# The second expert layer's weights and tokens from expert 2 on: three products of fp32r halves, split on the chip, in place of one fp32 product

## The chip, the cores and the metric

The kernel runs on one core of a Trainium2 chip, as a single launch. The metric is the device time of that launch in microseconds (us). Before the change, three timed runs gave 1102.97, 1103.93 and 1105.5 us; their median is 1103.93 us.

A core has five engines that work side by side, each through its own list of instructions in order: PE (matrix products; its weight loads are shown apart as PEld), DVE (elementwise and reductions, the vector engine), ACT (elementwise, the scalar engine), POOL and SP (here mostly issuers of DMAs). They wait for one another through semaphores. PE writes its products to PSUM, eight banks of 128 partitions by 512 fp32 columns; all else stands in SBUF.

## What is computed

Three stages follow one another. Only the last is touched.

```
x = attention(q, k, v)                 # 4 x 12 heads x 448 x 64 -> x[1792, 768]
x = moe(x)                             # each token to the expert of its largest logit
# the third stage, moe2:
logits = x @ w_gate                    # [1792, 8]
# all 14336 pairs (token, expert) by falling logit; a pair is taken if the token
# is free and the expert has fewer than 224 tokens
for e in range(8):
    mask = assigned == e               # exactly 224 tokens
    h = np.maximum(x[mask] @ w1[e], 0.0)   # 224x768 @ 768x1024
    out[mask] = h @ w2[e]                  # 224x1024 @ 1024x768
```

All tensors are fp32, the weights of an expert are 3 MB + 3 MB.

## The kernel before

Attention takes the first third of the span, the first expert layer (`moe1`) the second, the assignment and the second expert layer (`moe2`, L1961) the last. Already in `moe1` every fp32 operand is split into two numbers of the type fp32r: a high half (`w1h`, `xh`: the operand rounded to fp32r, an ACT copy, L846) and a low half (`w1l`, `xl`: operand minus high half, a DVE subtraction, L847). A product is then the sum of three, high x high, high x low and low x high (L880 to L882, L908 to L911).

`moe2` used plain fp32 products, an instruction each, which stands in the trace as two PE records. It works through the eight experts in the order in which the assignment fills them. Per expert n:

- First layer: for each of 8 blocks f of 128 hidden units, 6 products (`acc`, L2076; k = 0..5, 128 weights columns by the 224 tokens `xtt`) add up in one of two PSUM banks, f % 2 (`product`), so that block f+2 needs the bank that block f has left. `relu` (L2080) is one ACT instruction, PSUM to `ht`.
- Second layer: for each half h of the tokens (112), 8 x 2 products of 384 columns (`gemm2`, L2090) add up in two banks. `store` (L2095, L2096) copies them out by ACT and scatters the rows by a POOL DMA; half 0 is stored at step t = 25 of the expert, half 1 at step t = 3 of the next.
- The next expert's rows are gathered by POOL (L2056), and transposed by PE in four `turn`s during the second layer (L2064; ACT copies them to `xtt`, L2068).
- Weights: `pump` (L2027) issues one DMA for each piece, 6 of 512 KB (first layer) and 8 of 384 KB (second), straight into one of two sets of fp32 buffers, `w1s` and `w2s`; the next expert's pieces go into the other set.

The order of the instructions is made while the program is built. A small model of the engines' clocks (`Pace`, with `work(engine, cost, not before)`) decides only between which products the steps of the assignment (`asn`, DVE and PE work on 128 partitions, to which all of L1615 to L1955 belong) are put. All of `experts` is written out twice, for two variants of the assignment, of which one runs.

Of the kernel before, what the change touches and what calls it, by code (L numbers as in the profile page):

```python
# [1411 lines left out]
CAP = N // E  # L1412
# [545 lines left out]
        return t  # L1958


def moe2(tc, consts, wt, x0, asn, w1, w2, y, out):  # L1961

# [7 lines left out]
    with ExitStack() as ctx:  # L1970
        ctx.enter_context(tc.manual_schedule())
        p2 = ctx.enter_context(tc.tile_pool(name="m2p", bufs=1, reuse_waits="tile"))
        ps = ctx.enter_context(tc.tile_pool(name="m2ps", bufs=1, space=PSUM))
        w1s, w2s = wt
# [5 lines left out]
        xt = p2.tile([128, KD, CAP], F32, name="xtt")  # L1980
        ht = p2.tile([128, KF, CAP], F32, name="ht")
# [40 lines left out]

        nload, firsts, seconds = 0, 0, 0

        there, done = {}, {}  # L2027
# [6 lines left out]
        def pump(most=None):  # L2034
            nonlocal nload
            while most is None or nload < most:
                n, first, k = piece(nload)
                if n >= len(regs) or n > (firsts if first else seconds) + 1:
# [7 lines left out]
                w, wd = (w1, FF) if first else (w2, DM)  # L2046
                clock["d"] = max(clock["d"], clock["p"] + DELAY, choice[n]) + wd * 1.43e-3
                there[n, first, k] = clock["d"]
                nc.sync.dma_start(out=r, in_=w[bass.ds(regs[n], 1), 128 * k : 128 * (k + 1), :].rearrange("a p f -> p (a f)"))
                nload += 1  # L2050

        def gather(n, h):
            clock["d"] = max(clock["d"], work("g", 1.03) + GATHER) + 0.97
# [4 lines left out]
        def turn(g, px=px0):  # L2058
# [8 lines left out]
            there["x", h, i] = work("s", 0.45, t)  # L2067
            nc.scalar.activation(xt[dst], px, AF.Copy)  # L2068

        def acc(n, pg, f, k, shared=False):  # L2070
            fs = slice(128 * f, 128 * f + 128)
            check = dict(skip_group_check=shared)

            t = max(there[n, True, k], there["x", 0, k // 3], there["x", 1, k // 3])
            done[f] = work("p", 0.378, t)
            nc.tensor.matmul(pg, lhsT=w1s[n % 2][:, k, fs], rhs=xt[:, k, :], start=k == 0 and not (shared and f % 2), stop=k == KD - 1, **check)  # L2076

        def relu(pg, f):
            there["h", f] = work("s", 0.38, done[f])
            nc.scalar.activation(ht[:, f, :], pg, AF.Relu)  # L2080

        def gemm2(n, h, t):
            ts = slice(h * CP, (h + 1) * CP)

            todo = [(0, 0), (0, 1)] if t == 0 else [(1, 0), (1, 1)] if t == 1 else [(0, t), (1, t)]
            for i, k in todo:
                po = result(n, h, i)
                work("p", 0.646, max(there[n, False, k], there["h", k]))
                cs = slice(384 * i, 384 * i + 384)
                nc.tensor.matmul(po, lhsT=ht[:, k, ts], rhs=w2s[n % 2][:, k, cs], start=k == 0, stop=k == KF - 1)  # L2090

        def store(n, h):
            work("s", 0.98)
# [12 lines left out]
        nc.gpsimd.memset(w1s[0][0:1, FIRST, 0:1], 0.0)  # L2106
        few = nc.values_load(asn.regs[0:1, E : E + 1], engines=tuple(ALL), min_val=0, max_val=1)
        start = nload, known, list(regs), dict(asn.__dict__)

        def experts(compact):  # L2110
            nonlocal nload, known, firsts, seconds
            nload, known = start[:2]
            firsts, seconds = 0, 0
            regs[:] = start[2]
            choice[:] = [0.0]
            fetched.clear()
            asn.__dict__.update(start[3])
            there.update(((0, True, k), 0.0) for k in range(FIRST))
            pace.start(phases(compact), g=2.0, d=3.5)
            ready.update({0: 4.5, 1: 5.5})  # L2120
            pump()
            turns = [turn(g, (po3 + pg2)[g]) for g in range(4)]
# [6 lines left out]
            for n in range(E):  # L2129
                turns, gathered, turned = [], 0, 0  # L2130

                def ahead(t):

                    nonlocal gathered, turned
                    if n + 1 == E:
                        return
                    if known > n + 1 and gathered < 2:
                        gather(n + 1, gathered)
                        gathered += 1
                    elif t >= 17:  # L2140
                        if turned < 4 and gathered > turned // 2 and ready[turned // 2] <= clock["p"]:
                            if len(turns) == turned:
                                turns.append(turn(turned))
                                next(turns[turned])
                                return
                            for _ in turns[turned]:
                                pass
                            turned += 1

                for t in range(32):  # L2150
                    if n and t % 2 == 0 and 2 <= t <= 16:
                        relu(product(t // 2 - 1), t // 2 - 1)
                    if n and t == 3:
                        store(n - 1, 1)
                    if t == 25:
                        store(n, 0)
                    ahead(t)
                    pump()
                    if t < 16:
                        if n:  # L2160
                            f, a = divmod(t, 2)
                            for k in range(3 * a, 3 * a + 3):
                                acc(n, product(f), f, k)
                        elif t < 6:
# [11 lines left out]
                        if t == 15:  # L2176
                            firsts = n + 1
                    else:
                        gemm2(n, (t - 16) // 8, t % 8)
                seconds = n + 1  # L2180
                if n + 1 == E:
                    break
                while known <= n + 1:
                    clock["p"] = max(clock["p"], pace.step[2])
                    pace.emit()
                pump()
                while turned < 4:
                    if gathered > turned // 2:
                        clock["p"] = max(clock["p"], ready[turned // 2])
                    ahead(17)  # L2190
            store(E - 1, 1)

        with tc.If(few > 0):
            experts(True)
# [6 lines left out]
SLACK = 0.3  # L2201
AHEAD = 0.5
DELAY = 3.2
GATHER = 1.7
FIRST = 1
NHR = 5
# [12 lines left out]
def fused_kernel(tc, q, k, v, g_q, g_k, modality_id, w_gate, bias, w1, w2, w_gate2, w12, w22, out):  # L2219
    nc = tc.nc  # L2220
    with ExitStack() as ctx:
# [31 lines left out]
        wp3 = ctx.enter_context(tc.tile_pool(name="wp3", bufs=1, reuse_waits="tile"))  # L2253
        w1s = [wp3.tile([128, DM // 128, FF], F32, name=f"w1s{i}") for i in range(2)]
        w2s = [wp3.tile([128, FF // 128, DM], F32, name=f"w2s{i}") for i in range(2)]
        moe2(tc, consts, (w1s, w2s), x0, asn, w12, w22, y, out)
# [23 lines left out]
```

## Time and profile before

| what | us |
|---|---|
| median of three runs | 1103.93 |
| profiled execution, its own time | 1102.77 |
| its span (first to last instruction on the core) | 1101.0 |
| PE busy in the span | 1043.8 (95%) |
| DVE busy | 468.5 (43%) |
| ACT busy | 420.9 (38%) |
| mean granted TensorE clock, share of 2.4 GHz | 0.966 |

The profile is one execution, so durations taken from it add up to its span; its own time is 1.77 us above the span, and 1.16 us below the median. Busy shares are means over the three stages, and each stage is to be read by itself; the rows further below are from the stretches that matter here.

### The profile page before, as it was taken

The numbers are of one execution on the slowest core, as the hardware profiler recorded it, in microseconds if no ns is written. First come the engines' busy times: TensorE is split into PE (matmuls) and PEld (weight loads), VectorE is DVE, ScalarE is ACT, GpSimd is POOL, SyncE is SP. The second block draws the span as 40 slices with busy tenths as digits, with TensorE's granted clock in tenths as the row PEclk, the third lists the DMA queues.
The fourth block names the chain that finished last, engine by engine and source line by source line (L and its number), as shares of the span: only waits on it lengthen the run. The fifth ranks groups of instructions, "written<-read, shape, count | busy, mean of one in ns | idle before, by whom it ended". The sixth has DMA issues, their size and how long they took to land. (4 is left out here: it accounts for less than half of the span.)

```text
span 1101.0 us, 18184 instructions
## 1 busy us (share of the span) xinstructions
PE 1043.8 (95%) x6032; PEld 769.6 (70%) x6032; DVE 468.5 (43%) x1460; ACT 420.9 (38%) x995; POOL 233.5 (21%) x228
## 2 busy tenths in 40 slices
PE   7999999999999699999999997859999999999995
PEld 6555556556555688888888986657575886787782
DVE  5777877877875831111311112767777000000000
ACT  3677777677675322122532212721121111111110
POOL 4443333334333500100241101010101011001000
PEclk8899999999999899999999998959999999999998
DMA  6566566565365144627701101055752565376100
GB/s 157 128 145 145 129 149 150 126 156 144 81 175 179 30 147 157 221 97 260 259 22 46 45 30 51 11 181 209 261 196 61 221 229 212 130 251 216 38 13 27
DMA packets 80893, 150.99 MB, mean 137 GB/s; under 512 B 14254, under 2 KB 53422, under 8 KB 80752
## 3 DMA queue, kind: packets, MB, share of 16 engines
q1 hardware_dynamic: 75552, 126.06, 37.5%
q0 software_dynamic: 5200, 23.33, 6.7%
q8 instruction: 54, 0.88, 0.4%
q14 instruction: 87, 0.71, 0.2%
HBM read 110.69 MB, written 17.44 MB: 116 GB/s over the span
## 5 line engine op out<-in xcount | busy, mean ns | idle before, releaser
L2090 PE MATMUL bank<-w2s,ht 128*112 128x384 f32 x512 | 176.5, 490 | 0.0
L2076 PE MATMUL bank<-xtt,w1s 128*128 128x224 f32 x768 | 156.5, 358 | 0.0
L2076 PEld LDWEIGHTS bank<-xtt,w1s 128*128 128x128 f32 x768 | 143.4, 191 | 5.2 <-issue 1.2
L205 DVE TENSOR_REDUCE nm<-sp 112x1 f32<-112x448 f32 x192 | 117.9, 619 | 58.1 <-PE sp L204 29.6
L211 ACT ACTIVATE e<-sp,nm 112x448 f32<-112x448 f32 x192 | 121.8, 634 | 53.2 <-DVE nm L205 34.1
L2090 PEld LDWEIGHTS bank<-w2s,ht 128*112 128x112 f32 x512 | 86.2, 177 | 59.4 <-issue 1.1
L219 PE MATMUL tp<-ident,e 112*112 112x112 f32 x768 | 111.7, 269 | 0.6 <-DVE et L222 0.6
L219 PEld LDWEIGHTS tp<-ident,e 112*112 112x112 f32 x768 | 81.7, 135 | 26.2 <-issue 19.5
L232 PE MATMUL op<-et,qkv 112*64 112x448 f32 x384 | 99.4, 564 | 0.0
L225 ACT ACTIVATE et<-tp 112x448 f32<-112x448 f32 x144 | 78.4, 546 | 37.8 <-PE tp L219 36.3
L2080 ACT ACTIVATE ht<-bank 128x224 f32<-128x224 f32 x64 | 22.4, 357 | 173.0 <-PE bank L2076 166.7
L200 PE MATMUL sp<-bt,at 128*112 128x448 f32 x188 | 85.3, 454 | 1.6 <-DMA bt<-cut 1.6
L908 PE MATMUL po<-w2h,hh 128*128 128x384 f32 x240 | 85.7, 357 | 0.1
L880 PE MATMUL pg<-w1h,xh 128*128 128x512 f32 x180 | 75.9, 422 | 7.1 <-PEq L1192 5.8
L909 PE MATMUL po<-w2l,hh 128*128 128x384 f32 x240 | 81.7, 341 | 0.6 <-DVEq L837 0.5
L911 PE MATMUL po<-w2h,hl 128*128 128x384 f32 x240 | 80.5, 340 | 0.0
L2096 POOL DMA_INDIRECT out_dram<-x,ids x16 | 16.9, 1054 | 294.1 <-ACT x L2095 273.3
L882 PE MATMUL pg<-w1h,xl 128*128 128x512 f32 x180 | 72.2, 401 | 0.0
L881 PE MATMUL pg<-w1l,xh 128*128 128x512 f32 x180 | 72.0, 400 | 0.0
L137 POOL TENSOR_TENSOR xn<-qkv,rr 112x512 f32<-112x512 f32 x47 | 48.0, 1053 | 112.3 <-DVE rr L128 112.3
L200 PEld LDWEIGHTS sp<-bt,at 128*112 128x112 f32 x188 | 33.8, 180 | 48.5 <-issue 31.7
L896 DVE TENSOR_TENSOR hl<-ph,hh 128x512 fp32r<-128x512 f32 x30 | 20.7, 690 | 80.6 <-ACT hh L893 48.8
(417 smaller groups left out, 1550.3 us busy)
## 6 DMA issues: line engine op xcount, KB each, us to landing
w1s<-in_moe_w_dram SPq DMA_DIRECT2D x48, 512.0 KB
w2s<-in_moe_w_dram SPq DMA_DIRECT2D x64, 384.0 KB
qkv<-in_moe_w_dram SPq DMA_DIRECT2D x40, 384.0 KB
raw<-in_moe_w_dram SPq DMA_DIRECT2D x24, 512.0 KB
bt<-cut SPq DMA_DIRECT2D x96, 112.0 KB
at<-cut SPq DMA_DIRECT2D x96, 112.0 KB
qkv<-in_v_dram SPq DMA_DIRECT2D x12, 448.0 KB
xs<-xp SPq DMA_DIRECT2D x24, 224.0 KB
```

The costliest lines, as they stand in the source:

```text
L200: nc.tensor.matmul(sp, lhsT=at[:, h, cs], rhs=bt[:, h, :], start=h == 0, stop=h == 1)
L205: nc.vector.tensor_reduce(out=st["nm"][:, n : n + 1], in_=sp, axis=AX.X, op=OP.max, negate=True)
L211: nc.scalar.activation(e, st.pop(("s", n)), AF.Exp, bias=st["nm"][:, n : n + 1], accum_out=st["sm"][:, n : n + 1])
L219: nc.tensor.transpose(tp[:, kc, :], e[:, kc * CP : (kc + 1) * CP], ident[:CP, :CP])
L225: nc.scalar.activation(dst, tp, AF.Copy)
L232: nc.tensor.matmul(st["op"][h * D : (h + 1) * D, :], lhsT=raws[i // 2][:, 2, 2 * (i % 2) + h, kc * D : (kc + 1) * D], rhs=st["et"][:, h, k ...
L880: nc.tensor.matmul(pg, lhsT=xh[:, k, :], rhs=w1h[:, k, fs], start=k == 0, stop=False)
L908: nc.tensor.matmul(po[n], lhsT=hh[:, k, :], rhs=w2h[:, kk, cs], start=kk == 0, stop=False)
L909: nc.tensor.matmul(po[n], lhsT=hh[:, k, :], rhs=w2l[:, kk, cs], start=False, stop=False)
L911: nc.tensor.matmul(po[n], lhsT=hl[:, k, :], rhs=w2h[:, kk, cs], start=False, stop=kk == KF - 1)
L2076: nc.tensor.matmul(pg, lhsT=w1s[n % 2][:, k, fs], rhs=xt[:, k, :], start=k == 0 and not (shared and f % 2), stop=k == KD - 1, **check)
L2090: nc.tensor.matmul(po, lhsT=ht[:, k, ts], rhs=w2s[n % 2][:, k, cs], start=k == 0, stop=k == KF - 1)
```

## The change

For experts 0 and 1 of the sequence (`NAT = 2`) all stays as it was, but that their tiles are now allocated within `experts`. From expert 2 on:

- A weight piece is loaded into one of six raw buffers (`raws`, memory left over from the earlier stages), and `split` makes its halves: an ACT copy (h) and a DVE subtraction (l). `w1h`, `w1l`, `w2h`, `w2l` exist once, not twice: those of the next expert's first layer are written during the second layer of the current one, after its `store` of half 0; pieces 0 and 1 of the second layer behind them; pieces 2 to 7 during the first layer, one at each even step t. `pump` loads up to six pieces ahead of the splits.
- The tokens are split too: `turn` has a DVE subtraction more. High and low half lie side by side in `xx`, 448 columns for each k.
- First layer: `acc2` issues two products for each (f, k): `w1h` by all 448 columns, `w1l` by the 224 high ones. `relu2` then adds the two halves of the bank and makes the halves of the result: ACT copies the second half out (`hr`), DVE adds the first half to it, ACT writes `hh` = relu, DVE writes `hl`. The bank is left once DVE has added.
- Second layer: three products in place of one.
- The load of the very first piece, which had been issued before the branch, now comes behind it with the others.

```diff
+        raws = [t[:, FF * i : FF * i + FF] for t in qkv for i in range(3)]
+        xx = p2.tile([128, KD, 2, CAP], F32R, name="xx")
+        xh, xl = xx[:, :, 0, :], xx[:, :, 1, :]
+        hl = p2.tile([128, KF, CAP], F32R, name="hl")
...
         def product(f):
-            return pg2[f % 2][:, :CAP]
+            return pg2[f % 2][:, : 2 * CAP]
...
-            while most is None or nload < most:
+            while nload < max(direct, nsplit + direct + 6):
...
-                r = (w1s if first else w2s)[n % 2][:, k, :]
+                r = ws[n][0 if first else 1][:, k, :] if n < NAT else raws[(nload - direct) % 6][:, :wd]
...
+        def split(n, first, k):
...
+            nc.scalar.activation(h[:, k, :], r, AF.Copy)
+            there[n, first, k] = work("v", 0.08 + wd * 1.11e-3, t)
+            nc.vector.tensor_tensor(out=l[:, k, :], in0=r, in1=h[:, k, :].bitcast(F32), op=OP.subtract)
...
-            nc.scalar.activation(xt[dst], px, AF.Copy)
+            nc.scalar.activation((rows["xt"] if n < NAT else xh)[dst], px, AF.Copy)
+            if n >= NAT:
+                there["x", h, i] = work("v", 0.45, t)
+                nc.vector.tensor_tensor(out=xl[dst], in0=px, in1=xh[dst].bitcast(F32), op=OP.subtract)
...
+        def acc2(n, pg, f, k):
...
+            nc.tensor.matmul(pg, lhsT=h[:, k, fs], rhs=xx[:, k].rearrange("p a c -> p (a c)"), start=k == 0, stop=False)
+            nc.tensor.matmul(pg[:, :CAP], lhsT=l[:, k, fs], rhs=xh[:, k, :], start=False, stop=k == KD - 1)
+
+        def relu2(pg, f):
+            hr, hh = rows["hr"][f % NHR], rows["hh"]
...
+            nc.scalar.activation(hr, pg[:, CAP:], AF.Copy)
...
+            nc.vector.tensor_tensor(out=hr, in0=pg[:, :CAP], in1=hr, op=OP.add)
...
+            nc.scalar.activation(hh[:, f, :], hr, AF.Relu)
...
+            nc.vector.scalar_tensor_tensor(hl[:, f, :], hr, 0.0, hh[:, f, :].bitcast(F32), op0=OP.max, op1=OP.subtract)
...
+                if n < NAT:
+                    nc.tensor.matmul(po, lhsT=ht[:, k, ts], rhs=ws[n][1][:, k, cs], start=k == 0, stop=k == KF - 1)
+                else:
+                    w2h, w2l = wh["2"]
+                    nc.tensor.matmul(po, lhsT=hh[:, k, ts], rhs=w2h[:, k, cs], start=k == 0, stop=False)
+                    nc.tensor.matmul(po, lhsT=hh[:, k, ts], rhs=w2l[:, k, cs], start=False, stop=False)
+                    nc.tensor.matmul(po, lhsT=hl[:, k, ts], rhs=w2h[:, k, cs], start=False, stop=k == KF - 1)
...
-            if len(regs) == 1:
-                pump(most=FIRST)
...
+                        if t % 2 and arrival and nload > nsplit + direct and arrival[piece(nsplit + direct)] <= clock["p"] + EARLY:
+                            k = next(splits, None)
+                            if k is not None:
+                                split(n + 1, True, k)
...
+                        relu(product(f)[:, :CAP], f) if n < NAT else relu2(product(f), f)
+                    if n >= NAT and t % 2 == 0 and t // 2 + 2 < KF:
+                        split(n, False, t // 2 + 2)
...
-                                acc(n, product(f), f, k)
+                                acc(n, product(f)[:, :CAP], f, k) if n < NAT else acc2(n, product(f), f, k)
...
+                for k in splits:
+                    split(n + 1, True, k)
+                if n + 1 >= NAT:
+                    split(n + 1, False, 0)
+                    split(n + 1, False, 1)
...
+EARLY = 0.3
+NHR = 5
+NAT = 2
```

What it makes of the order on ACT, from the second layer of expert 3 into the first layer of expert 4. Before, the copies of the transposed tokens (L2068), the stores (L2095) and the relus (L2080), `ht` being the hidden units:

```order
L2068 ACTIVATE xtt<-bank_11371 128x3x112 x4
L2095 ACTIVATE x_89<-bank_11368 112x384
L2095 ACTIVATE x_89<-bank_11369 112x384
L2080 ACTIVATE ht<-bank_11366 128x224
L2095 ACTIVATE x_89<-bank_11370 112x384
L2095 ACTIVATE x_89<-bank_11368 112x384
L2080 ACTIVATE ht<-bank_11367 128x224
L2080 ACTIVATE ht<-bank_11366 128x224
```

After, at the same place; `qkv_87` and `qkv_88` are raw buffers, L2142 is the store, L2063 the high halves, L2110 and L2114 the two ACT steps of `relu2`:

```order
L2085 ACTIVATE xx<-bank_11364 128x3x112 x4
L2142 ACTIVATE x_89<-bank_11363 112x384
L2142 ACTIVATE x_89<-bank_11361 112x384
L2063 ACTIVATE w1h<-qkv_87 128x1024
L2063 ACTIVATE w1h<-qkv_88 128x1024 x3
L2063 ACTIVATE w1h<-qkv_87 128x1024 x2
L2063 ACTIVATE w2h<-qkv_87 128x768
L2063 ACTIVATE w2h<-qkv_88 128x768 x2
L2110 ACTIVATE hr_12573<-bank_11359 128x224
L2114 ACTIVATE hh<-hr_12573 128x224
L2063 ACTIVATE w2h<-qkv_88 128x768
L2142 ACTIVATE x_89<-bank_11362 112x384
```

Nine copies of weights stand between the store of half 0 and the first hidden block of the next expert, and one more between each of the blocks that follow, up to the sixth.

DVE, before, in the last second layer in which it has work, that of expert 1 (steps of the assignment; `table`, `ids`: the token lists of an expert):

```order
L1853 TENSOR_SCALAR g_10960<-i_10945,k 128x112 x7
L1861 TENSOR_TENSOR table<-table,bank_11365 112x32
L1862 TENSOR_TENSOR sel<-table,full 112x32
L1863 TENSOR_REDUCE sum_10981<-sel 112x4
L1865 TENSOR_TENSOR ids<-sum_10981 112x2
L1897 TENSOR_SCALAR fe<-rem 128x8
```

After, the same steps, in the second layer of expert 2, among the low halves of expert 3's weights (L2065):

```order
L1853 TENSOR_SCALAR g_10960<-i_10945,k 128x112 x4
L2065 TENSOR_TENSOR w1l<-qkv_87,w1h 128x1024
L2065 TENSOR_TENSOR w1l<-qkv_88,w1h 128x1024
L1861 TENSOR_TENSOR table<-table,bank_11358 112x32
L1862 TENSOR_TENSOR sel<-table,full 112x32
L1863 TENSOR_REDUCE sum_10981<-sel 112x4
L1865 TENSOR_TENSOR ids<-sum_10981 112x2
L2065 TENSOR_TENSOR w1l<-qkv_88,w1h 128x1024
L1897 TENSOR_SCALAR fe<-rem 128x8
```

The last steps of the assignment have moved one expert further, and stand in one queue with the splits.

And DVE in the first layer of expert 4, where it had nothing before (L2112 the addition that leaves the bank, L2116 `hl`):

```order
L2065 TENSOR_TENSOR w2l<-qkv_88,w2h 128x768 x2
L2065 TENSOR_TENSOR w2l<-qkv_87,w2h 128x768
L2112 TENSOR_TENSOR hr_12573<-bank_11359,hr_12573 128x224
L2116 SCALAR_TENSOR_TENSOR hl<-hr_12573,hh 128x224
L2065 TENSOR_TENSOR w2l<-qkv_87,w2h 128x768
L2112 TENSOR_TENSOR hr_12574<-bank_11360,hr_12574 128x224
L2116 SCALAR_TENSOR_TENSOR hl<-hr_12574,hh 128x224
```

Each addition stands behind the subtraction of one weight piece, three before the first.

## Rows read from the trace of the kernel before

**Rows 1.** Page, section 2: busy tenths of 40 slices of the span
```profile
PE   7999999999999699999999997859999999999995
DVE  5777877877875831111311112767777000000000
```

**Rows 2.** Chain of waits, experts 2 and 3: start us, us, what
```profile
849.69 3.41 PE bank L2076 x18
...
890.08 18.16 PE bank L2076 x96
...
909.53 0.29 PE bank L2064 x3
```

**Rows 3.** Stretches: expert 3's two layers, the end; columns in the first line
```profile
core 0: us, PE busy (x) PEld busy (x) DVE busy (x) ACT busy (x) POOL busy (x), PEclk, DMA share, GB/s
890.08:908.24 18.16, 18.16 (x97) 18.15 (x97) 0.00 (x0) 3.26 (x9) 0.97 (x1) 1.00 0.61 225
908.24:930.04 21.80, 21.80 (x77) 12.34 (x77) 0.00 (x0) 3.14 (x7) 2.94 (x4) 1.00 0.49 162
1088.75:1101.00 12.25, 0.00 (x0) 0.00 (x0) 0.00 (x0) 0.49 (x1) 0.94 (x1) 0.72 0.10 30
```

**Rows 4.** Timeline of PE in moe1: start us, us, line, out<-in, shape, count
```profile
607.39 0.34 PE L908 MATMUL po<-w2h,hh 128*128 128x384 f32 x1
...
610.52 0.33 PE L908 MATMUL po<-w2h,hh 128*128 128x384 f32 x1
...
611.03 1.40 PE L979 MATMUL pl<-wgt,xtm 128*128 128x8 f32 x12
...
612.84 0.39 PE L882 MATMUL pg<-w1h,xl 128*128 128x512 f32 x1
...
614.94 0.39 PE L882 MATMUL pg<-w1h,xl 128*128 128x512 f32 x1
```

**Rows 5.** Groups by line and shape, ACT: count | busy us, mean ns
```profile
L2080 ACT ACTIVATE ht<-bank 128x224 f32<-128x224 f32 x64 | 22.4, 357 | 173.0 <-PE bank L2076 166.7 <-issue 6.4
...
L846 ACT ACTIVATE w1h<-raw 128x512 fp32r<-128x512 f32 x12 | 6.5, 623 | 0.3 <-ACTq L837 0.3
...
L854 ACT ACTIVATE w2h<-qkv 128x768 fp32r<-128x768 f32 x8 | 6.1, 835 | 0.0
```

**Rows 6.** Timeline of ACT, six copies in a row
```profile
534.06 3.23 ACT L846 ACTIVATE w1h<-raw 128x512 fp32r<-128x512 f32 x6 [0.27 <-ACTq L837]
```

**Rows 7.** Group and single line, DVE subtractions (ns min/median/max)
```profile
L847 DVE TENSOR_TENSOR w1l<-raw,w1h 128x512 fp32r<-128x512 f32 x12 | 7.4, 684 | 0.2 <-ACT w1h L846 0.2
...
L1033 DVE TENSOR_TENSOR w2l<-qkv,w2h x1: 936/936/936, 380.1 to 380.1; 128x768 fp32r<-128x768 f32 x1
```

**Rows 8.** Timeline, DVE subtractions in a row and a POOL DMA issue
```profile
536.94 3.70 DVE L847 TENSOR_TENSOR w1l<-raw,w1h 128x512 fp32r<-128x512 f32 x6 [0.24 <-ACT w1h L846]
...
537.48 1.04 POOL L984 DMA_INDIRECT y<-yr,ti  x1 [23.78 <-POOLq L837]
...
543.10 3.70 DVE L847 TENSOR_TENSOR w1l<-raw,w1h 128x512 fp32r<-128x512 f32 x6
```

**Rows 9.** Timeline, ACT to DVE hand-over
```profile
604.30 0.60 ACT L893 ACTIVATE hh<-ph 128x512 fp32r<-128x512 f32 x1 [3.23 <-PE ph L890]
...
604.93 0.69 DVE L896 TENSOR_TENSOR hl<-ph,hh 128x512 fp32r<-128x512 f32 x1 [3.12 <-ACT hh L893]
```

**Rows 10.** Stretch of the assignment's last steps (columns as in Rows 3)
```profile
846.94:848.53 1.59, 1.59 (x6) 0.86 (x6) 1.42 (x11) 0.00 (x0) 0.00 (x0) 1.00 0.00 0
```

**Rows 11.** Timeline of SP and PE, start of the second expert layer
```profile
724.10 9.79 SPq L2049 DMA_DIRECT2D w1s<-in_moe_w_dram  x6
...
741.73 1.78 PE L2076 MATMUL bank<-xtt,w1s 128*128 128x224 f32 x4
```

**Rows 12.** Stretches at the two clocks (columns as in Rows 3)
```profile
580.00:600.00 20.00, 18.26 (x102) 15.97 (x102) 4.45 (x8) 4.60 (x8) 1.44 (x2) 1.00 0.13 43
...
360.00:380.00 20.00, 12.23 (x57) 11.42 (x56) 19.16 (x61) 5.28 (x11) 9.56 (x7) 0.74 0.00 0
```

More of the change, by code (lines that the diff above doesn't have):

```diff
@@ L1958, in compact, with moe2 @@
         return t
-def moe2(tc, consts, wt, x0, asn, w1, w2, y, out):
+def moe2(tc, consts, qkv, x0, asn, w1, w2, y, out):
     nc = tc.nc
@@ L2021, in moe2 @@
         clock, work = pace.clock, pace.work
-        nload, firsts, seconds = 0, 0, 0
-        there, done = {}, {}
+        nload, nsplit, direct = 0, 0, NAT * (KD + KF)
+        ws, wh = {}, {}
+        there, done, arrival = {}, {}, {}
         fetched = []
@@ L2045, in pump @@
                     nc.gpsimd.memset(r[0:1, 0:1], 0.0)
-                w, wd = (w1, FF) if first else (w2, DM)
                 clock["d"] = max(clock["d"], clock["p"] + DELAY, choice[n]) + wd * 1.43e-3
-                there[n, first, k] = clock["d"]
+                (there if n < NAT else arrival)[n, first, k] = clock["d"]
                 nc.sync.dma_start(out=r, in_=w[bass.ds(regs[n], 1), 128 * k : 128 * (k + 1), :].rearrange("a p f -> p (a f)"))
                 nload += 1
+        def split(n, first, k):
+            nonlocal nsplit
+            assert piece(nsplit + direct) == (n, first, k) and (n, first, k) in arrival
+            h, l, wd = (*wh["1"], FF) if first else (*wh["2"], DM)
+            r = raws[nsplit % 6][:, :wd]
+            t = work("s", 0.1 + wd * 9.3e-4, arrival[n, first, k])
+            nc.scalar.activation(h[:, k, :], r, AF.Copy)
+            there[n, first, k] = work("v", 0.08 + wd * 1.11e-3, t)
+            nc.vector.tensor_tensor(out=l[:, k, :], in0=r, in1=h[:, k, :].bitcast(F32), op=OP.subtract)
+            nsplit += 1
+            pump()
         def gather(n, h):
@@ L2100, in moe2, with tiles @@
             pace.emit()
-            if len(regs) == 1:
-                pump(most=FIRST)
         for h in range(2):
             gather(0, h)
-        nc.gpsimd.memset(w1s[0][0:1, FIRST, 0:1], 0.0)
         few = nc.values_load(asn.regs[0:1, E : E + 1], engines=tuple(ALL), min_val=0, max_val=1)
-        start = nload, known, list(regs), dict(asn.__dict__)
+        start = known, list(regs), dict(asn.__dict__)
         def experts(compact):
[L2111 to L2114, printed above, removed]
+            nonlocal nload, nsplit, known
+            nload, nsplit, known = 0, 0, start[0]
+            regs[:] = start[1]
+            there.clear()
+            arrival.clear()
             choice[:] = [0.0]
-            fetched.clear()
-            asn.__dict__.update(start[3])
-            there.update(((0, True, k), 0.0) for k in range(FIRST))
+            fetched[:] = [(0, 0), (0, 1)]
+            asn.__dict__.update(start[2])
             pace.start(phases(compact), g=2.0, d=3.5)
             ready.update({0: 4.5, 1: 5.5})
+            room = [ExitStack() for _ in range(NAT)]
+            def tiles(n, side, *what):
+                pool = room[n].enter_context(tc.tile_pool(name="m2w" + what[0][0], bufs=1, reuse_waits="tile", side=side))
+                return [pool.tile([128, *shape], dt, name=name) for name, shape, dt in what]
+            for n, side in enumerate(("left", "right")):
+                ws[n] = tiles(n, side, (f"w1s{n}", (KD, FF), F32), (f"w2s{n}", (KF, DM), F32))
+            rows["xt"], rows["ht"] = tiles(1, "right", ("xtt", (KD, CAP), F32), ("ht", (KF, CAP), F32))
+            nc.gpsimd.memset(ws[0][0][0:1, FIRST, 0:1], 0.0)
             pump()
-            turns = [turn(g, (po3 + pg2)[g]) for g in range(4)]
+            turns = [turn(0, g, (po3 + pg2)[g]) for g in range(4)]
             for g in turns:
@@ L2129, in experts @@
             for n in range(E):
+                splits = iter(range(KD) if NAT <= n + 1 < E else ())
                 turns, gathered, turned = [], 0, 0
@@ L2175, in experts @@
                                 relu(first_product(i), i)
-                        if t == 15:
-                            firsts = n + 1
                     else:
                         gemm2(n, (t - 16) // 8, t % 8)
-                seconds = n + 1
                 if n + 1 == E:
                     break
+                if n < NAT:
+                    room[n].close()
+                if n == 0:
+                    wh["1"] = tiles(0, "left", *((i, (KD, FF), F32R) for i in ("w1h", "w1l")))
+                elif n == 1:
+                    wh["2"] = tiles(1, "right", *((i, (KF, DM), F32R) for i in ("w2h", "w2l")))
+                    rows["hh"], *rows["hr"] = tiles(1, "right", ("hh", (KF, CAP), F32R), *((f"hr{i}", (CAP,), F32) for i in range(NHR)))
                 while known <= n + 1:
@@ L2190, in experts @@
                     ahead(17)
+                pump()
+                for k in splits:
[3 more added lines that the diff above has]
+                    split(n + 1, False, 1)
             store(E - 1, 1)
+            for r in room:
+                r.close()
         with tc.If(few > 0):
@@ L2252, in fused_kernel @@
         weights.close()
[L2253 to L2256, printed above, removed]
+        moe2(tc, consts, qkv, x0, asn, w12, w22, y, out)
 _INS = ["q", "k", "v", "g_q", "g_k", "moe_modality_id", "moe_w_gate", "moe_modality_bias", "moe_w1", "moe_w2", "moe2_w_gate", "moe2_w1", "moe2_w2"]
```

33 lines of the change are left out of this document (20 added, 13 removed).

## Prediction, on record before the changed kernel ran

> **What bounds the kernel now.** I read the page's slices first: PE is at 9 of 10 in nearly all of the last third, while DVE falls to nothing in its last nine slices [rows 1]. The chain of waits then says whether that busy PE is the path: from expert 2 (849.69 us) on it names nothing but PE, product after product, with the four transposes of 0.29 us between [rows 2]. The stretches of one expert give the sizes [rows 3]: its first layer is 18.16 us, filled by 48 products (18.16 / 48 = 0.378 us each), its second 21.80 us, of which 4 x 0.29 = 1.16 us are transposes and 20.64 us the 32 products (0.645 us each). An expert takes 39.96 us, and in it ACT works 6.4 us and DVE nothing. So PE time saved there is saved at the end, as long as ACT and DVE can feed the new products. Behind the last product lie 12.25 us of copy, scatter and exit [rows 3], which the change leaves alone.
>
> **The second layer.** Each fp32 product becomes three fp32r products of 384 columns. In `moe1` eighteen of these start within 610.52 - 607.39 = 3.13 us, so 0.174 us each [rows 4]. 96 x 0.174 = 16.70 us stand against 20.64: 3.94 us saved per expert, six times. `hl` and `w2l` are later inputs of the same products; they are ready long before (below), so I add nothing for waits.
>
> **The first layer on PE.** Per (f, k) there is one product of 448 columns and one of 224. From nine products of 512 columns within 614.94 - 612.84 = 2.10 us, 0.233 each [rows 4], and the 384-column ones, the slope is 0.059 / 128 columns, which puts 448 at 0.204 us. The 224-column fp32r product is not in the trace. From below the same slope gives 0.100; a product also loads 128 columns of weights, and the twelve 8-column products at 611.03, which are hardly more than loads, take 1.40 / 12 = 0.117 us each [rows 4]; from above, the fp32 product of the same shape takes 0.378. I take 0.117, since 384 and 512 columns lie on one line and nothing bends it but the load. A block f is then 6 x (0.204 + 0.117) = 1.92 us and the layer 15.4 us, if nothing is waited for.
>
> **What PE waits for there.** Block f+2 needs the bank that DVE's addition of block f leaves, and DVE and ACT now have splits in the same queues. I follow them through one expert, from the start of a second layer at 0.
>
> - ACT stores half 0 when its products are done, at 48 x 0.174 + 1.16 = 9.5; its second copy (0.49 us, the ACT time in the last stretch of [rows 3]) ends at 10.03.
> - Then six copies of 1024 columns. Copies of 512 and 768 take 0.623 and 0.835 us [rows 5], so 1024 takes 1.05; in a row they follow at 0.10 less than their length ((3.23 - 0.623) / 5 = 0.52 [rows 6]). The first ends at 11.08.
> - DVE's subtractions: 0.684 and 0.936 us for 512 and 768 [rows 7], so 1.19 for 1024 and 0.40 for 224; in a row they follow at 0.08 less ((3.70 - 0.684) / 5 = 0.60 [rows 8]). A hand-over from ACT to DVE costs 0.03 (604.30 + 0.60 to 604.93 [rows 9]). DVE is the slower of the two: six low halves end at 11.11 + 5 x 1.11 + 1.19 = 17.85, just when the first layer starts (16.70 + 1.16 = 17.86; PE needs the sixth only 5 x 0.32 later). Three low halves of `w2` at 0.86 and the addition (0.40) end at 20.8. The first bank is left 2.9 us into the layer, where PE would want it after 3.84: no wait yet.
> - From then on the queues go round block by block: addition 0.40, hand-over 0.03, relu on ACT 0.28 (0.36 [rows 5] less the overlap), copy of a weight piece 0.835, hand-over 0.03, its subtraction 0.86: 2.43 us, against PE's 1.92. In the first round the store of half 1 lies in the ACT queue: 2.58. Block 5 leaves its bank at 2.9 + 2.58 + 4 x 2.43 = 15.2, block 7 starts then and ends at 17.2. Blocks 6 and 7 have no split between and do not add.
>
> So the first layer takes 17.2 us, 1.8 of it waits, against 18.16. Expert by expert 17.2 + 17.86 = 35.06 against 39.96: 4.9 us saved.
>
> **The other edits.** The six raw buffers are filled as subtractions free them: the pieces of the next `w1` take those that `w2` pieces 2 to 7 leave in the first layer (the last some 13 us in), and are wanted 10 us into the second, over ten us later; a stretch with such loads moves 162 to 225 GB/s [rows 3], and 6 MB in 35 us is 180: I cost it at nothing, with the bound that each expert waits 1 to 2 us for its first piece (+6 to +12 in all). The load that now starts behind the branch shifts six loads of `w1` by one; the first was issued at 724.10, and PE begins at 741.73 [rows 11], so its cover is 17 us and I cost it at nothing (bound: +2). POOL issues as before. The DVE subtraction of each `turn` lies in the second layer, where DVE is idle until the splits. What does cost: expert 2's halves of `w2` cannot be written until expert 1's second layer is through (they lie in its memory), so its three stand inside the first layer: 0.83 + 0.03 + 3 x 0.86 + 0.40 = 3.8 instead of 2.9, +0.9. And the last steps of the assignment now stand between the splits of expert 3, 846.94 to 848.53 of before, ten steps in 1.59 us [rows 10]: +1.5; four short ones by expert 4's, some 0.6. Together 3.0. PE does the assignment's few small products there, too, 0.3.
>
> **The sum**, against the profiled execution. Expert 2 starts at 849.69; six first layers of 17.2 (103.2), six second layers of 16.70 (100.2), five rounds of transposes (5.8), 3.0 and 0.3 bring the last product to 1062.2, where it ended at 1088.75: -26.5. The execution took 1102.77 us and the median of the runs is 1.16 above it: 1103.93 - 26.5, **1077 us**.
>
> **Where the range comes from.** If everything on ACT and DVE hid (first layer 15.4, no steps in the way), the gain grows by 6 x 1.8 + 3 to 1063.5. If no overlap between neighbours in a queue came true (1.19 and 0.94 for subtractions, hl's 0.4 partly in the round, 2.75 a round and the first bank at 3.6), block 5 would leave its bank at 17.5 and the layer take 19.4: +2.2 x 6, 1091.
>
> The subtractions have two operands in SBUF and POOL issues three or four DMAs per expert, of about 1 us. In the trace such an issue (537.48) falls into one stretch of six subtractions and none of its kind into the stretch at 543.10: both take 3.70 us [rows 8], so I charge nothing. The Trainium skill, "SBUF — State Buffer", section "SBUF: two separate sides", has DVE with two SBUF inputs and a GpSimd operation that reads SBUF lock each other out for a whole instruction; by that rule up to 3 us per expert would come on top, 1095, and the equal 3.70 us speak against it for DMA issues.
>
> **Rivals.**
>
> - *The queues decide more than I think* (ACT and DVE become the bound; raw pieces late): 1084 to 1096, the working above. For it: two engines pass each block four times to and fro; against: the hand-over of 0.03 us.
> - *The queues hide*: 1063 to 1070, if the round is 2.0 us rather than 2.43. Against: the subtraction of 0.86 and the copy of 0.835 alone are 1.7.
> - *The 224-column product is slow* (the slower side): if it costs what the fp32 one costs, 0.378, a pair is 0.582 and the layer 27.9 us, hiding the queues: 6 x 10.7 - 3 = +61, 1138. The change loses from the point where the first layer takes 17.2 + 26.5 / 6 = 21.6 us, that is a pair of 0.45 and a small product of 0.246 us. For it: the rows have no fp32r product of so few columns; against: the line through 384 and 512.
> - *The clock falls* (slower too): at 1.2 GHz the 15.4 us of products would double, 30.8 instead of 17.2: +13.6 x 6 - 3, 1156. With PE busy 12.23 of 20 us the granted clock was 0.74, with 18.26 of 20 it was 1.00 [rows 12]. The new first layer is busy 15.4 of 17.2, 90%, about the latter. The Trainium skill, "TensorE: Matmul & The Clock Gate", section "A second HAM failure mode: psum-queue depth-cycling", tells of a kernel in which PE idled briefly while its banks cycled, and the clock swung between its levels; here two banks cycle just so. By that rule the time is this rival's; the row at 91% busy speaks against it.
>
> **Chances.** Forecast (1070 to 1084) 0.62; queues longer 0.17; queues hidden 0.08; slow small product 0.07; clock 0.03; gains and losses that happen to cancel 0.03. The range 1064 to 1094 leaves out the two slow rivals, the cancelling case and the far ends of the queue cases. A change of under 0.2% (2.2 us) can't be told from none: faster 0.86, same 0.03, slower 0.11.
>
> **What would show it.** In the profile after: the second layer of an expert at 17.9 us with 0.174 from product to product; the pair of the first layer at 0.32; PE idle 0.4 to 0.5 us before each block from the third or fourth on, released by DVE's addition; additions about 2.4 us apart; no wait of ACT's first `w1` copy for a DMA; clock 1.00 to the end. A pair above 0.45 us, or a first layer above 21.6 us, would make the forecast wrong in sign; idle PE at the start of a layer, waiting for a weight piece, would show a cost I left out.

## The result, and the profile after

The changed kernel took 1090.08 us (median of four runs, 1087.67 to 1091.4), the kernel before 1103.45 beside it: a ratio of 0.9878, interval 0.9865 to 0.9892. That is 13.4 us gained where 26.5 were forecast. The profiled execution took 1089.45 us, span 1087.5; its last product ends at 1075.20 us in place of the forecast 1062.2, so 13.0 us are to be found, and all of them stand between expert 2's start (849.49, forecast 849.69) and that end.

The page's slices of the changed kernel, as in [rows 1], with the clock: DVE is now at work to the end, and PE has lost its even 9s; the clock dips, too.

```profile
PE   7999999999999699999999998949999999999895
...
DVE  5776877877875931111322121585778766565470
...
PEclk7899999999999899999999999867999999899998
```

Stretches of the changed kernel, columns as in [rows 3]: expert 3's two layers, the first layers of experts 4 and 7, and the tail.

```profile
886.98:907.40 20.42, 17.90 (x98) 15.93 (x98) 13.80 (x24) 10.56 (x23) 1.04 (x2) 0.92 0.88 288
907.40:925.33 17.93, 17.93 (x111) 17.52 (x110) 10.61 (x24) 10.07 (x15) 3.40 (x3) 1.00 0.32 96
925.33:946.57 21.24, 18.75 (x98) 17.16 (x98) 13.26 (x23) 10.87 (x23) 1.04 (x2) 0.84 0.86 280
...
1040.80:1058.46 17.66, 16.47 (x98) 14.51 (x98) 12.48 (x23) 10.26 (x23) 0.94 (x1) 1.00 0.38 132
...
1075.20:1087.50 12.30, 0.03 (x1) 0.00 (x0) 0.00 (x0) 0.57 (x2) 0.94 (x1) 0.61 0.10 31
```

The second layer is where it was forecast: 17.93 us, filled by PE, against 21.80 [rows 3]. The first layer is not: 20.42 and 21.24 us against a forecast of 18.7 (expert 3) and 17.8 (expert 4) and 18.16 before, so in these experts it has become slower than the fp32 one. Of the six only that of expert 7, the last, is faster than before (17.66). (A stretch runs to the modelled end of the layer's last product, some 0.15 us longer than from start to start, as in the table below.) The tail is the same.

The chain of waits in expert 3 (start us, us, what) shows the forecast round, and ahead of it something else.

```profile
874.05 0.17 PE bank L2135
874.23 0.17 PE bank L2136
874.40 0.18 PE bank L2137
...
884.12 6.46 DMA qkv<-in_moe_w_dram
...
890.67 0.85 ACT w2h L2063
891.54 0.96 DVE w2l L2065
892.50 0.31 DVE hr L2112
...
895.00 0.40 DVE hr L2112
895.42 0.39 ACT hh L2114
895.81 0.74 ACT w2h L2063
896.58 0.96 DVE w2l L2065
897.54 0.31 DVE hr L2112
...
905.82 0.21 PE bank L2104
906.04 0.10 PE bank L2105
```

Products of 0.174 us, a pair of 0.315 (0.21 + 0.10; forecast 0.204 + 0.117), rounds as forecast (additions end at 892.81, 895.40 and 897.85: 2.59 us with the store in between, then 2.45). But before the first addition the chain stands in a load of a raw piece of `w2`, 6.46 us from issue to landing, and the first bank is left at 892.81, 5.8 us into the layer in place of 2.9 + 1.5.

### The profile page after: what moved, and what is told of

It reads as the page before. It is cut to its first block, busy times and chain, and to the rows that moved or that the text cites. A ratio compares the mean times of both kernels' runs of the same rounds, so it can differ in the third digit from the quotient of the medians.

```text
span 1087.5 us, 19047 instructions
## 1 busy us (share of the span) xinstructions
PE 1016.0 (93%) x6224; PEld 785.1 (72%) x6224; DVE 601.5 (55%) x1664; ACT 506.6 (47%) x1127; POOL 238.3 (22%) x228
## 5 line engine op out<-in xcount | busy, mean ns | idle before, releaser
L2104 PE MATMUL bank<-xx,w1h 128*128 128x448 f32 x288 | 101.9, 403 | 13.9 <-DVE hr L2112 13.8
L2105 PE MATMUL bank<-xx,w1l 128*128 128x224 f32 x288 | 79.1, 275 | 0.0
L2104 PEld LDWEIGHTS bank<-xx,w1h 128*128 128x128 f32 x288 | 57.2, 198 | 26.3 <-DVE hr L2112 21.2
L2143 POOL DMA_INDIRECT out_dram<-x,ids x16 | 17.2, 1074 | 254.3 <-ACT x L2142 129.3
L2135 PE MATMUL bank<-w2h,hh 128*112 128x384 f32 x192 | 66.3, 345 | 0.0
L2137 PE MATMUL bank<-w2h,hl 128*112 128x384 f32 x192 | 64.7, 337 | 0.0
```

What stands on the lines that cost most here:

```text
L2104: nc.tensor.matmul(pg, lhsT=h[:, k, fs], rhs=xx[:, k].rearrange("p a c -> p (a c)"), start=k == 0, stop=False)
L2105: nc.tensor.matmul(pg[:, :CAP], lhsT=l[:, k, fs], rhs=xh[:, k, :], start=False, stop=k == KD - 1)
L2135: nc.tensor.matmul(po, lhsT=hh[:, k, ts], rhs=w2h[:, k, cs], start=k == 0, stop=False)
L2137: nc.tensor.matmul(po, lhsT=hl[:, k, ts], rhs=w2h[:, k, cs], start=False, stop=k == KF - 1)
```

## Experiments

All layers below are read from PE's timeline, from the first product of the layer to the first of the next (us). The start of expert 0 wanders by some 5 us between executions (737.9 to 743.5, by the stages ahead, which the edits leave alone but for the place of two tiles in e4, e9 and e10), so small differences between medians are read from the layers.

| kernel | median us | ratio to before, interval | first layers, experts 2 to 7 |
|---|---|---|---|
| changed | 1090.08 | 0.9878 (0.9865 to 0.9892) | 19.1 20.3 21.1 19.3 20.8 17.5 |
| e1, short loads | 1079.44 | 0.9785 (0.9769 to 0.9802) | 19.1 18.7 18.0 17.4 17.5 17.5 |
| e2, short splits | 1072.26 | 0.9715 (0.9698 to 0.9731) | 19.1 16.2 17.0 16.0 16.0 15.2 |
| e3, gathers later | 1078.67 | 0.9771 (0.9752 to 0.9790) | 19.1 18.7 18.0 17.5 17.5 17.5 |
| e4, two places | 1077.39 | 0.9762 (0.9742 to 0.9782) | 19.1 18.7 18.0 17.4 17.5 17.5 |
| e5, w2 later | 1088.71 | 0.9877 (0.9860 to 0.9893) | 17.7 17.5 17.4 17.4 17.4 17.4 |
| e6, w2l on POOL | 1079.81 | 0.9794 (0.9778 to 0.9811) | 16.6 21.5 17.6 17.0 17.3 18.6 |
| e7, four banks | 1073.65 | 0.9736 (0.9720 to 0.9752) | 19.1 18.6 18.0 15.2 15.2 15.2 |
| e8, e6 + e7 | 1075.76 | 0.9769 (0.9749 to 0.9788) | 16.7 18.9 17.6 15.2 15.2 15.2 |
| e9, e3 + e4 + e7 | 1069.48 | 0.9697 (0.9683 to 0.9711) | 19.1 18.6 18.0 15.2 15.2 15.2 |
| e10, e9 from expert 4 | 1067.74 | 0.9690 (0.9669 to 0.9711) | 19.1 18.6 15.2 15.2 15.2 15.2 |

**e1, short loads of w2.**

```diff
-                nc.sync.dma_start(out=r, in_=w[bass.ds(regs[n], 1), 128 * k : 128 * (k + 1), :]...)
+                cols = SHORT if n >= NAT and not first else wd    # SHORT = 96
+                nc.sync.dma_start(out=r[:, :cols], in_=w[bass.ds(regs[n], 1), 128 * k : 128 * (k + 1), :cols]...)
```

> From expert 2 on, each load of a second-layer piece brings 96 of its 768 columns (48 KB in place of 384); the splits still work on 768, the rest of a buffer being what lay there, so the output is not the reference's. Measured in the changed kernel: the six first layers take 19.3, 20.4, 21.2, 19.4, 21.0 and 17.7 us, the first bank is left 4.7, 5.8, 6.4, 4.8, 6.4 and 3.5 us into them, and ACT's first copies of w2 wait for loads. Theory A (the first three pieces of w2 land late, because their buffers come free only when w1 is split, and the load then takes 5 to 7 us): the first addition comes 3 to 3.5 us into each layer, the layers take 17.5 us (18.4 for expert 2), the profiled execution 1079 to 1080 against 1089.45, the clock stays at 1.00. Theory B (ACT and DVE are simply slower together than their single durations, or DVE and POOL share a port): nothing moves, 1089. Theory C (the clock, 0.84 to 0.92 in three of the layers, costs the time by itself): 1089 and the clock as low as before.

Theory A holds: 17.4 to 17.5 us in experts 5 to 7, the clock 0.965 over the span (changed kernel: 0.958). ACT's wait for loads, from expert 2 into expert 7 (850 to 1040 us), in the changed kernel:

```profile
ACT w2h L2063 <- DMA qkv<-in_moe_w_dram: 15.2, 12, 2.6
```

and here (850 to 1030 us; us in total, times, longest):

```profile
ACT w2h L2064 <- DMA qkv<-in_moe_w_dram: 1.8, 2, 1.2
```

Experts 2 to 4 stay above the 17.5 us that theory A gave them: 19.1, 18.7 and 18.0, in e3 and e4 too. What is left there is not the loads'. For experts 3 and 4 it has the size that the prediction set down for the steps of the assignment in DVE's queue (17.2 + 1.5 and 17.2 + 0.6); that it is these steps was not tried by itself.

**e2, short splits of w2.**

```diff
-            r = raws[nsplit % 6][:, :wd]
+            cols = wd if first or n == NAT else SHORT    # SHORT = 96
+            r = raws[nsplit % 6][:, :cols]
```

(`h` and `l` are cut to `cols` as well.)

> All loads as in the changed kernel, but from expert 3 on the splits of second-layer pieces work on 96 of 768 columns (ACT and DVE some 0.25 us each in place of 0.83 and 0.96), so the output is not the reference's. If the round of ACT and DVE (2.45 us a block) is what PE waits for after the first bank, it shrinks to some 1.2 us, below PE's 1.89, and a layer takes 15.3 us where the loads are in time; theory A leaves the wait for the third piece of w2, which stands in ACT's queue before the first hidden block, so that block 2 starts some 5 us into the layer: 16.5 us, five layers 82 in place of 99.7, execution 1071 to 1074. If the loads cost nothing: 15.3 us each, 1066. If the rounds are not what PE waits for: 1086 to 1089.

16.0 to 17.0 us with the loads as late as ever, 15.2 in expert 7, which has no late load: the round is the bound behind the first bank, the loads are ahead of it, and PE's own need is 15.2.

**e3, gathers later.** Only the place of two POOL DMAs changes.

```diff
-                    if known > n + 1 and gathered < 2:
+                    if known > n + 1 and gathered < 2 and (n < NAT or t >= GLATE):    # GLATE = 4
```

> The gathers of the next expert's rows (two POOL DMAs) stand behind the scatter of half 1 in POOL's queue, so they start some 7 us into the first layer in place of 2 to 4 us after half 0 is stored, when the first w2 pieces are being loaded. If it is the competition with the gathers that makes those loads take 5 to 7 us: the first bank is left 2 us earlier in experts 3 to 6, execution 1081 to 1083. If the loads are slow by what else is in flight (each other, the scatter) or merely issued late: 1088 to 1090. Turns of the next expert could start later, if the gathers land after the layer's end; I expect not, they have 10 us.

More than I expected: the layers are those of e1. In expert 6 of the changed kernel the two gathers (L2073) go out on POOL while ACT wants the first pieces of `w2` (timeline rows, with the idle time ahead and what ended it):

```profile
995.81 1.49 POOL L2073 DMA_INDIRECT xg<-y,ids  x1 [0.30 <-issue]
997.60 1.96 POOL L2073 DMA_INDIRECT xg<-y,ids  x1 [0.30 <-issue]
```

```profile
1001.24 0.85 ACT L2063 ACTIVATE w2h<-qkv 128x768 fp32r<-128x768 f32 x1 [1.29 <-DMA qkv<-in_moe_w_dram]
1003.51 0.84 ACT L2063 ACTIVATE w2h<-qkv 128x768 fp32r<-128x768 f32 x1 [1.43 <-DMA qkv<-in_moe_w_dram]
1006.27 0.84 ACT L2063 ACTIVATE w2h<-qkv 128x768 fp32r<-128x768 f32 x1 [1.91 <-DMA qkv<-in_moe_w_dram]
```

In e3 the same gathers follow the scatter, and the three copies follow one another:

```profile
999.76 0.96 POOL L2143 DMA_INDIRECT out_dram<-x,ids  x1 [11.74 <-ACT hr L2110]
1001.02 0.95 POOL L2073 DMA_INDIRECT xg<-y,ids  x1 [0.30 <-DMA qkv<-in_moe_w_dram]
1002.28 0.95 POOL L2073 DMA_INDIRECT xg<-y,ids  x1 [0.30 <-issue]
```

```profile
992.87 0.85 ACT L2063 ACTIVATE w2h<-qkv 128x768 fp32r<-128x768 f32 x1 [0.41 <-DMA qkv<-in_moe_w_dram]
994.21 0.85 ACT L2063 ACTIVATE w2h<-qkv 128x768 fp32r<-128x768 f32 x1 [0.49 <-DMA qkv<-in_moe_w_dram]
995.29 0.85 ACT L2063 ACTIVATE w2h<-qkv 128x768 fp32r<-128x768 f32 x1 [0.23 <-PE bank L2105]
```

The time from issue to landing says the same, as the median of eight loads in 13 us around expert 3's start (KB each, us to landing); the changed kernel:

```profile
qkv<-in_moe_w_dram SPq DMA_DIRECT2D x8, 384.0 KB, 5.4
```

and e3:

```profile
qkv<-in_moe_w_dram SPq DMA_DIRECT2D x8, 384.0 KB, 3.9
```

**e4, two landing places.** To make room, two tiles of `moe1` move into a pool that is closed before `moe2`.

```diff
+        spare = [p2.tile([128, DM], F32, name=f"spare{i}") for i in range(2)]
...
+            if KD <= j < KD + 2:
+                return None, spare[j - KD]
```

> Two more landing buffers, for pieces 0 and 1 of the second layer alone, so that they are loaded behind w1 during the first layer before, and only pieces 2 to 7 wait for a buffer that w1 leaves. Piece 2 is then loaded first after w1's first split, some 4 us before the first layer starts. Theory A: the first bank is left 3 to 3.5 us into the layers, they take 17.5 us (expert 2: 18.4), execution 1079 to 1081, the clock 1.00. Theory B: 1089.

The layers of e1 and e3 again, and ACT never waits for a load in experts 3 to 6. So three different edits (fewer bytes, no gathers at that time, an earlier load) take away the same 9.8 us of first layers (118.1 to 108.2 in each). What they have in common is that the pieces land in time. The clock is back at 1.00 in all three as well, but that is worth 0.3 us (further below).

**e5, the halves of w2 behind their own blocks** (with e3's edit).

```diff
-                    if n >= NAT and t % 2 == 0 and t // 2 + 2 < KF:
-                        split(n, False, t // 2 + 2)
+                    if n >= NAT and t % 2 == 0 and 2 <= t <= 16:
+                        split(n, False, t // 2 - 1)
...
-                if n + 1 >= NAT:
-                    split(n + 1, False, 0)
-                    split(n + 1, False, 1)
```

> The late gathers of e3, and the splits of w2 piece f stand behind the hidden block f (0 to 7) in place of three pieces ahead of the first block and one behind each of the next five. In e3 the first bank is left 4.7, 4.2, 3.5 us into experts 2 to 4 and 3.0 in the others. If what delays it is the three subtractions of w2 behind those of w1 in DVE's queue: with none of them ahead it is left 2.7 to 2.9 us in, all layers take 17.1 us, and the execution 1073 to 1074 (e3: 1078.98). If rows of w2 come too late for the second layer, its first products wait: PE idle after the layer's end, 1076 to 1080. If the rounds of DVE and ACT are not the bound: no change, 1079.

None of the three expectations came true. The first layers are near the first one (17.4, with the first bank left 2.9 us in) and together 3.6 us shorter than in e3, but the second ones are 11.5 us longer. Expert 5's two layers:

```profile
964.95:982.32 17.37, 16.21 (x98) 14.35 (x97) 10.14 (x19) 9.33 (x21) 2.86 (x3) 1.00 0.80 245
982.32:1002.39 20.07, 18.19 (x111) 17.62 (x109) 12.10 (x17) 10.85 (x17) 1.05 (x2) 1.00 0.53 170
```

and the chain early in the second one:

```profile
986.36 0.96 DVE w2l L2065
987.32 0.43 DVE xx L2088
...
987.79 0.51 PE bank L2081 x3
```

Eight rounds in place of five: the last end 5 us into the second layer, the first transposed tokens wait behind them in DVE's queue, and the next transposes wait for their bank: PE is idle for 1.9 us there. It was not the missing rows of `w2` that I had named, but the tail of the rounds.

**e6, low halves of w2 on POOL** (with e3's edit).

```diff
-            nc.vector.tensor_tensor(out=l[:, k, :], in0=r, ...
+            (nc.vector if first else nc.gpsimd).tensor_tensor(out=l[:, k, :], in0=r, ...
```

> The late gathers of e3, and the low halves of w2 are subtracted by POOL in place of DVE (1.8 us each in the first expert layer's trace, eight per expert, 14.6 of 33 us). My theory of the round (addition 0.39, relu 0.28, copy 0.83, subtraction 0.96, one after the other 2.45 us a block, against 1.89 of PE) then leaves addition, relu and copy, 1.6 us: PE is not held up any more, layers of 15.3 to 15.6 us from expert 3 on, execution 1064 to 1067. The rival: POOL's subtraction and DVE's operations with two SBUF operands keep each other out (the Trainium skill, "SBUF — State Buffer", section "SBUF: two separate sides", says so); then an addition or a low half on DVE waits up to 1.8 us for POOL, rounds stay at 2.4 to 3.6 us, 1078 to 1090.

The rival: 1079.81, nothing gained on e3, though DVE has 0.96 us less per block. Groups of experts 3 to 7 in e6 (count | busy us, mean ns):

```profile
L2065 POOL TENSOR_TENSOR w2l<-qkv,w2h 128x768 fp32r<-128x768 f32 x40 | 79.7, 2011 | 32.5 <-DMA qkv<-in_moe_w_dram 23.1 <-ACT w2h L2063 8.0 <-issue 1.1
L2116 DVE SCALAR_TENSOR_TENSOR hl<-hr,hh 128x224 fp32r<-128x224 f32 x40 | 46.4, 1159 | 18.3 <-ACT hh L2114 18.3
...
L2112 DVE TENSOR_TENSOR hr<-bank,hr 128x224 f32<-128x224 f32 x40 | 15.3, 383 | 18.9 <-ACT hr L2110 18.8
```

and of the changed kernel:

```profile
L2116 DVE SCALAR_TENSOR_TENSOR hl<-hr,hh 128x224 fp32r<-128x224 f32 x40 | 15.7, 392 | 18.3 <-ACT hh L2114 18.3
```

`hl`, with both operands in SBUF, goes from 392 to 1159 ns; the addition, with one of them in PSUM, stays at 383. One by one it is as clear: the 26 of the 40 `hl` that meet a subtraction on POOL took 0.52 to 3.99 us, the 14 others 0.39 each, while the 21 additions that meet one took 0.38 to 0.39. Of expert 3's 21.5 us the trace shows that the first bank is left 6.1 us into the layer; why so late was not followed further.

**e7, four banks from expert 5** (with e3's edit).

```diff
-        def product(f):
-            return pg2[f % 2][:, : 2 * CAP]
+        def product(f, n=0):
+            return (pg2 + bank[:2] if n >= FOUR else pg2)[f % (4 if n >= FOUR else 2)][:, : 2 * CAP]    # FOUR = 5
```

> The late gathers of e3, and in the first layers of experts 5 to 7 the hidden blocks go round four PSUM banks in place of two (the two of the assignment, which is over by then). If PE waits there only for the bank that an addition leaves, it no longer waits for the second block before it but the fourth: layers of 15.2 to 15.4 us in experts 5 to 7 (e3: 17.5), execution 1072 to 1073. The halves of block f are then ready later than the bank order demanded, but the second layer needs block 7 only 7 us in. If ACT's and DVE's rounds bound the layer by themselves (the second layer waits for its halves), PE idles in the second layer instead: 1076 to 1079.

15.2 us in all three, without idle PE. Expert 5's first layer in e3, then in e7:

```profile
959.07:976.53 17.46, 16.28 (x98) 14.36 (x97) 12.35 (x22) 9.86 (x23) 2.94 (x4) 1.00 0.98 302
```

```profile
960.86:976.04 15.18, 15.18 (x97) 14.34 (x97) 11.09 (x19) 8.95 (x20) 2.96 (x4) 1.00 0.99 310
```

The wait was for the bank. The second layers of experts 5 and 6 are 0.4 and 0.6 us longer (18.4 and 18.5), still a clear gain.

**e8, e6 and e7 together.**

> e6 and e7 together. If POOL relieves the rounds, the banks add nothing: as e6, 1064 to 1067. If POOL and DVE keep each other out, the banks hide it in experts 5 to 7: between e6 and e6 less 6 us, and the second layers of those experts begin with PE waiting for halves.

The banks hide the slowed DVE in the first layers (15.2), and the second layers of experts 5 and 6 are longer (19.7 and 19.9, with PE idle for 1.3 and 1.0 us early in them): the second expectation.

**e9 and e10, the best of these together**, e10 with `FOUR = 4`.

> The late gathers of e3, the two landing buffers of e4 and the four banks of e7 from expert 5. e3 took 1078.98 in its profiled execution, e4 gave the same layers as e3, e7 takes three first layers from 17.5 to 15.2 us. If late landings were one cause, removed by either of e3 and e4, the two together add nothing: as e7, 1072 to 1074. If each removed a part of its own: 1069 to 1071.

> As e9, with four banks already from expert 4, in whose layer the assignment still uses two of them for its last small products. If the layer of expert 4 (18.0 us) waits for banks like those behind it: 15.3 to 16 us, execution 2 to 2.7 us under e9. If the shared banks make products wait for the assignment's readers: no gain or a loss of a few us.

e9's layers are e7's, all six; of the 5.9 us between the two profiled executions (1068.80 and 1074.72) 5.5 lie ahead of expert 0, which starts at 737.9 us here and at 743.4 in e7. So e4's edit adds nothing to e3's, as expected of one cause, though the time by itself would speak for the other expectation; whether the earlier start is chance or the moved tiles is open. e10 shortens expert 4's first layer from 18.0 to 15.2 and lengthens its second from 18.4 to 19.4, 1.8 us gained by the layers where 2 to 2.7 were expected. Both beat the kernel before by 3% and the changed one by some 2%; between the two the intervals overlap.

## Why the prediction came out so

**The direction and the rounds were right**, step by step. Second layer: 0.174 us a product, 17.86 forecast, 18.0 to 18.4 measured from start to start; the excess, 1.4 us over six layers, is mostly the assignment's products and their places. First layer on PE: 15.4 forecast, 15.2 measured without waits (e7). The small product, unknown before, took 0.10 us: the slope of the 512 and 384 columns alone, so the weight loads did not show, and nothing of the fp32 price. The round of ACT and DVE: 2.43 forecast, 2.45 measured; the layer under it 17.2 forecast, 17.5 measured where no load is late. The cover of the load behind the branch held: expert 0 starts at 742.45 us (741.73 before) and its first layer takes 27.7 us (27.6).

**The number**: the gain forecast was twice the one that came. The 1090 us lie inside the range of 1064 to 1094, but outside the forecast of 1070 to 1084; they lie where the first rival had its time (1084 to 1096). That rival named late raw pieces, but its time was worked out from longer rounds (2.75 us) in every expert, and these did not come, so that it fits is luck. Luck, too, is that the +6 to +12 us by which the refill was bounded cover what it cost: they were meant for the first piece of `w1`, and ACT never waits for a load of `w1`. Of the 13.0 us by which the last product is late, 9.8 are late landings, 1.0 is expert 2 (19.1 for 18.1), 0.9 the first layers of experts 5 to 7 (17.5 for 17.2) and 1.4 the second layers; 0.1 is left over.

**The step that failed** is the one that cost the refill of the raw buffers at nothing, with a bound of 1 to 2 us per expert. It cost 9.8 us of first layers (118.1 against 108.2 in e3): 1.6 to 3.3 us in each of experts 3 to 6. I had followed the pieces of `w1`, which do come in time, and not the first three of `w2`: their buffers come free only as DVE splits `w1` (issues at 881.08, 882.21 and 884.12 us for expert 3), and ACT wants them from 884.5 on, when it is through with `w1`. And "POOL issues as before" looked at DVE's port alone: the gathers of the next rows, harmless while weights went straight into a second set of buffers, now go out just then (880.39 and 882.18) and share the DMA engines with the loads. The two gathers and the three loads as they go out in the changed kernel:

```profile
880.39 1.49 POOL L2073 DMA_INDIRECT xg<-y,ids  x1 [0.30 <-PE bank L1858]
882.18 0.95 POOL L2073 DMA_INDIRECT xg<-y,ids  x1 [0.30 <-PE bank L2137]
```

```profile
881.08 0.33 SPq L2054 DMA_DIRECT2D qkv<-in_moe_w_dram  x1
...
882.21 0.33 SPq L2054 DMA_DIRECT2D qkv<-in_moe_w_dram  x1
...
884.12 0.33 SPq L2054 DMA_DIRECT2D qkv<-in_moe_w_dram  x1
```

The 225 GB/s of a first layer before [rows 3] were an average over 18 us and say nothing of the 5 us in which two gathers and three pieces are all due.

**Expert 2** was late by 1.9 us, not 0.9, and for another reason: ACT writes the first `w2h` in e3 at 845.29 while PE is in expert 1's second layer until 848.51, so that memory was free. What is late is DVE, which has steps of the assignment between its splits (its last low half of `w1` ends at 850.3 there, after that layer's end, and those of `w2` follow at once). This is read from the trace and was not tried by itself.

**The clock** did fall, as a rival had it, but only behind the long waits. In expert 4 PE stood idle for 2.4 us before 931.69 and then worked at half clock (stretches of the changed kernel):

```profile
929.00:931.69 2.69, 0.28 (x2) 0.00 (x1) 1.49 (x3) 1.10 (x3) 0.00 (x0) 0.91 1.03 402
931.69:937.90 6.21, 6.21 (x21) 5.78 (x22) 3.82 (x8) 4.72 (x10) 0.96 (x1) 0.50 0.92 306
```

Its price is small: by the rounds the fourth addition would have ended at 931.65 + 2.58 + 2 x 2.45 = 939.13 us, and it ended at 939.47. In experts 3 and 6, with a clock of 0.92 over the layer, it cost nothing that can be seen: the first bank is left 1.6 and 3.3 us later than in e3, and the layers are 1.6 and 3.3 us longer. In e3, where PE waits at most 0.5 us for a bank, all six first layers have 1.00, with the same two banks in turn. The rule of the Trainium skill that I cited for that rival ("TensorE: Matmul & The Clock Gate", "A second HAM failure mode: psum-queue depth-cycling") does not show in e3's six layers.

Nor does the length of a wait alone tell. In e5 PE waits for 1.9 us in the second layer of each of experts 2 to 6; behind the wait in expert 2 the clock fell, behind the next ones it did not. The wait in expert 3, and what followed it (stretches of e5):

```profile
911.03:912.92 1.89, 0.00 (x1) 0.00 (x0) 1.50 (x3) 0.77 (x2) 0.00 (x0) 1.00 0.70 225
912.92:919.00 6.08, 6.08 (x39) 5.98 (x40) 1.57 (x5) 1.60 (x4) 0.00 (x0) 1.00 0.32 101
```

What decides it these runs do not show.

**The port.** That POOL's DMA issues cost DVE nothing was right: in the changed kernel, from expert 3's first layer on, the 25 low halves of `w1` took 1.22 to 1.23 us each, and during twelve of them POOL issued a DMA. The lock itself is real: the Trainium skill, "SBUF — State Buffer", "SBUF: two separate sides", gives it to DVE operations with two SBUF inputs against a GpSimd operation that reads SBUF, and e6 shows just this pair, and the addition from PSUM left alone.

## What to carry to other kernels

When weights no longer land in a second full set of buffers but pass through a few shared ones, ask of each piece when its buffer comes free, when it is wanted, and which other DMAs are due in between: an average bandwidth does not answer that. A chain of small steps on two engines is well foretold by adding single durations and hand-overs from the trace; to get PE out of it, more PSUM banks brought 2.3 us of a first layer, less 0.5 in the second. Shorter steps would bring as much (15.2 us in expert 7 of e2), but e2 gets them by leaving out work that the result needs, and neither moving the work to another engine (e6) nor into the next layer (e5) brought anything.

## Not expected of the hardware

A 384 KB load took 3.9 us to land among other loads and 5.4 with two gathers of 112 rows beside it (medians of eight, e3 and the changed kernel). A DVE operation of 0.39 us with both operands in SBUF took up to 3.99 us when it met a subtraction on POOL, 1.16 on average over all 40 of e6. After one wait of 2.4 us PE ran at the lower clock for 6.2 us, and after four waits of 1.9 us in e5 it did not.
